# Reordering two periods of an attention-plus-MLP kernel, and moving one transpose from TensorE to DMA

## The chip, the cores and the metric

The kernel runs on one core of one Trainium2 chip. The metric is the device time of one execution in microseconds. Executions agree within some 0.3%. The experiments were timed in five or six rounds against the kernel before, on the same chip, and a trace of one execution of each is read beside the times. In the text PE is TensorE, DVE is VectorE, ACT is ScalarE, POOL is GpSimd, SP is SyncE, whose queue issues DMAs here. PSUM is the memory that PE writes its results to, a bank a part of it.

## The reference

Attention of 8 heads with a window of 96 positions, 8 global positions and a linear bias, followed by a two-layer MLP whose activation is a scaled and shifted square of relu:

```python
scores = scale * np.matmul(q, k.transpose(0, 1, 3, 2))       # 4 x 8 x 768 x 768
keep = is_global | is_local                                  # 8 global, 96 local
scores = np.where(keep, scores + bias, -1e9)
a = softmax(scores)
x = (a @ v).transpose(0, 2, 1, 3).reshape(3072, 512)
r = np.maximum(x @ w_in, 0.0)                                # 512 -> 2048
out = (s * (r * r) + b) @ w_out                              # 2048 -> 512
```

(`softmax` stands for the reference's maximum, exponential and division.)

## The kernel before

The 3072 tokens are cut into 12 granules of 256. For each granule: loads by POOL (f32 to bf16), transposes of k and q by DMA, scores, exponentials, multiplication by a bias template, values, normalization, transpose of the result x to xT, first layer, square, second layer. The instruction order on each engine is written by hand. Granules 0 to 2 are a start; granules 3 and 4 go through `period`, and from granule 5 on `steady` repeats. P1(3,0) in the text is block 0 of granule 3's first layer, xT(3) is xT of granule 3. In the steady part the second layer is computed with 7 instead of 8 block products, for which differences of w_out (`W_tw`) and sums of activations (`W_sw`) are made on DVE.

```python
def XT_pe(j, eng="act", tag="pso"):         # x -> xT on PE, copied out by ACT
    ...
    nc.tensor.transpose(ps[...], xn[j][...], ident[:])     # 8 of them
    nc.scalar.copy(xT[j][:], ps[:])

def XT_dma(j):                              # x -> xT by two DMA transposes from SP
    for i in range(GB):
        nc.sync.dma_start_transpose(xT[j][:, :, i * P : (i + 1) * P], xn[j][:, i, :, :]...)

def XB(j):                                  # k and q of a granule, four DMA transposes from SP
    XBk(j); XBq(j)

def P1(j, fp, sq="dve", ...):               # one of 8 first-layer blocks: 8 matmuls, relu on ACT;
    ...                                     # the square on ACT, on DVE, or later on DVE by Q(j, fp)

def P2(j, c):                               # one of 8 second-layer blocks: 4 matmuls

def period(j, items, at, late=None, mid=()):               # granules 3 and 4
    SS(j, (0, 1))                           # scores, exponentials, multiplication of two head pairs
    run(items, at[0]); A(j, 0)              # A: values and normalization of a head pair
    run(items, at[1]); A(j, 1, "psh")
    run(list(mid), 100)
    SS(j, (2, 3))
    if j == 3:
        pace(pts[j, 2][0:1, 0, 0:1])        # POOL waits for the multiplied scores,
        load_granule(6)                     # then issues the six loads of granule 6
    ...
    VO(j + 1); XB(j + 2)
    if late is not None:
        run(items, 1); late(); XT_pe(j, "act", "psh")      # granule 3
```

`KO` and `VO` copy the k and v blocks of the next granule side by side, with the global positions put in.

The softmax here doesn't subtract the row's maximum and nothing guards it: scores larger than these inputs give would overflow.

## Time and profile before

| view | value |
|---|---|
| time, median of the 3 runs given first | 207.81 us (207.53 to 207.9) |
| span of the profiled execution | 205.9 us |
| busy: PE, DVE, ACT, POOL | 96%, 84%, 56%, 36% |
| scores of granule 5 start (PE timeline) | 76.05 us |

The DVE timeline of the kernel before (start in us, length in us, instruction): the two value copies made while POOL issues loads, and the same two one granule later, when it doesn't.

```profile
60.71 0.76 DVE L363 COPY vo<-vaug 128x1040 bf16<-128x1040 bf16 x1
61.50 0.83 DVE L366 COPY vo<-vaug 8x1040 bf16<-8x1040 bf16 x1
...
72.90 0.43 DVE L363 COPY vo<-vaug 128x1040 bf16<-128x1040 bf16 x1
73.37 0.43 DVE L366 COPY vo<-vaug 8x1040 bf16<-8x1040 bf16 x1
```

The same copy costs nearly twice as much at 61 us as at 73 us.

### The profile page before, as it was taken

How to read it: one execution, taken by the hardware profiler on the slowest of the kernel's cores; microseconds unless marked ns; L12 is line 12 of the kernel's file. 1: busy time of each engine (PE TensorE's matmuls, PEld its weight loads, DVE VectorE, ACT ScalarE, POOL GpSimd, SP SyncE). 2: the span in 40 equal slices, each digit the busy share in tenths (PEclk: the TensorE clock that was granted, in tenths of full speed). 3: DMA queues.
4: the chain of work that ended last, by engine and by line, in shares of the span. 5: the costliest groups of instructions: out<-in, count | busy, mean ns of one | idle time of the engine just before them, and what ended most of it. 6: DMA issues, size and time to landing. Idle time of an engine off the chain costs nothing.

```text
span 205.9 us, 5597 instructions
## 1 busy us (share of the span) xinstructions
PE 198.5 (96%) x2286; PEld 160.6 (78%) x2293; DVE 173.4 (84%) x415; ACT 115.9 (56%) x174; POOL 73.2 (36%) x98
## 2 busy tenths in 40 slices
PE   7988999999999999999999999999999999999993
PEld 2667776547766678988988988988988988988883
DVE  5897677699989989788799799788799799787693
ACT  5887588355878576536536536536446446424400
POOL 8993683848274019009009119019000000000000
PEclk9999999999999999999999999999999999999999
DMA  5999999999999969969999969999975140040022
GB/s 164 193 184 197 192 194 193 181 154 145 148 133 150 237 83 99 194 137 118 108 227 109 208 91 106 204 109 121 204 85 140 42 133 23 0 153 5 0 105 102
DMA packets 103962, 27.64 MB, mean 134 GB/s; under 512 B 91392, under 2 KB 102016, under 8 KB 103936
## 3 DMA queue, kind: packets, MB, share of 16 engines
q0 software_dynamic: 70976, 13.11, 83.5%
q1 hardware_dynamic: 31904, 13.64, 33.8%
q10 hardware_dynamic: 1056, 0.52, 0.9%
q8 instruction: 18, 0.29, 0.6%
q14 instruction: 8, 0.07, 0.2%
HBM read 27.26 MB, written 6.29 MB: 163 GB/s over the span
## 4 chain that ended last, share of the span: by engine, by line
PE 81%; DMA 5%; POOL 5%; DVE 4%; ACT 2%; issue 1%; SPq 0%; POOLq 0%; ACTq 0%
PE ps L552 37%; PE ps_w L735 15%; PE ps_wb L735 7%; PE ps L622 6%; PE ps_av L470 4%; PE ps_wa L735 4%; DMA w_in_bf<-in_moe_w_in_dram 4%; PE ps_s L414 4%; POOL vaug L112 2%; PE ps_2s L622 2%; DVE pt L441 2%; DMA xT<-xn 1%; DVE o_pr L660 1%; POOL w_in_bf L129 1%; ACT pt L427 1%
## 5 line engine op out<-in xcount | busy, mean ns | idle before, releaser
L552 PE MATMUL ps<-xT,w_in_bf 128*128 128x256 bf16 x768 | 96.5, 273 | 2.1 <-DMA w_in_bf<-in_moe_w_in_dram 1.2
L552 PEld LDWEIGHTS <-w_in_bf 128*128 128x128 bf16 x768 | 72.6, 98 | 13.0 <-DMA w_in_bf<-in_moe_w_in_dram 2.3
L570 ACT ACTIVATE gT<-ps 128x512 bf16<-128x512 f32 x72 | 43.1, 598 | 58.5 <-PE ps L552 56.4
L427 ACT ACTIVATE pt<-ps_s 128x1024 bf16<-128x1024 f32 (+1 forms) x48 | 43.0, 950 | 4.0 <-PE ps_s L414 4.0
L735 PEld LDWEIGHTS <-sw 128*128 128x128 bf16 x288 | 28.1, 98 | 3.4
L589 DVE TENSOR_TENSOR gT<-gT 128x512 bf16<-128x512 bf16 x73 | 27.6, 415 | 1.7 <-ACT gT L570 1.6
L112 POOL DMA_DIRECT2D vaug<-in_v_dram x24 | 21.6, 912 | 4.1 <-DMA w_out_bf<-in_moe_w_out_dram 1.7
L441 DVE TENSOR_TENSOR pt<-pt,tmpl 128x1024 bf16<-128x1024 bf16 x31 | 20.7, 686 | 2.1 <-ACT pt L427 2.1
L735 PEld LDWEIGHTS <-gT 128*128 128x128 bf16 x208 | 19.8, 98 | 3.2 <-issue 0.2
L488 DVE TENSOR_TENSOR xn<-ps_av,rc 128x256 bf16<-128x256 f32 x48 | 20.4, 424 | 1.7
L125 POOL COPY pdum<-xT 1x1 bf16<-1x1 bf16 x5 | 2.5, 509 | 50.5 <-DMA xT<-xn 50.5
L622 PE MATMUL ps<-w_out_bf,gT 128*128 128x512 bf16 x74 | 18.8, 379 | 0.4 <-issue 0.2
L735 PE MATMUL ps_w<-tw,sw 128*128 128x256 bf16 x144 | 18.7, 273 | 0.0
L745 DVE SCALAR_TENSOR_TENSOR u<-ps_w,s_bc,bvec 128x256 f32<-128x256 f32 x27 | 12.9, 479 | 6.4 <-PE ps_w L735 6.4
L470 PEld LDWEIGHTS <-pt 128*128 128x128 bf16 x352 | 15.4, 98 | 3.3 <-DVE pt L441 1.2
L568 ACT ACTIVATE gT<-ps 128x512 bf16<-128x512 f32 x23 | 13.6, 598 | 6.9 <-PE ps L552 6.7
L104 POOL DMA_DIRECT2D qnat<-in_q_dram x18 | 16.0, 904 | 2.8 <-DMA w_out_bf<-in_moe_w_out_dram 1.4
L104 POOL DMA_DIRECT2D knat<-in_k_dram x18 | 15.9, 892 | 1.8 <-issue 1.5
L470 PE MATMUL ps_av<-vaug,pt 128*128 128x65 bf16 x224 | 16.2, 193 | 0.2 <-DVE pt L441 0.2
L622 PEld LDWEIGHTS <-gT 128*128 128x128 bf16 x96 | 8.7, 97 | 8.1
L487 DVE RECIPROCAL rc<-ps_av 128x4 f32<-128x4 f32 x48 | 8.7, 181 | 6.6 <-PE ps_av L470 6.4
L414 PE MATMUL ps_s<-qT,kT 64*128 64x128 bf16 x224 | 12.5, 218 | 0.1
(102 smaller groups left out, 242.4 us busy)
## 6 DMA issues: line engine op xcount, KB each, us to landing
out_dram<-o_pr SPq DMA_DIRECT2D x10, 512.0 KB, 6.0
vaug<-in_v_dram POOLq DMA_DIRECT2D x24, 128.0 KB, 8.0
knat<-in_k_dram POOLq DMA_DIRECT2D x22, 128.0 KB, 6.5
qnat<-in_q_dram POOLq DMA_DIRECT2D x22, 128.0 KB, 8.0
w_in_bf<-in_moe_w_in_dram POOLq DMA_DIRECT2D x8, 256.0 KB, 8.3
w_out_bf<-in_moe_w_out_dram POOLq DMA_DIRECT2D x4, 512.0 KB, 9.8
out_dram<-o_pr SPq DMA_DIRECT2D x3, 256.0 KB, 2.5
raw<-in_q_dram ACTq DMA_DIRECT2D x2, 256.0 KB, 4.9
```

The lines of the kernel that those rows point to most:

```text
L104: nc.gpsimd.dma_start(t[:, i, :, :], src[b, :, sb * P : (sb + 1) * P, :].rearrange("h p d -> p h d"))
L112: nc.gpsimd.dma_start(vaug[b % 2][:, sb, :, 0:D], v[b, :, sb * P : (sb + 1) * P, :].rearrange("h p d -> p h d"),)
L414: nc.tensor.matmul(ps[:, hi, oc * P : (oc + 1) * P], lhsT=kt[r, :], rhs=qT[j][r, hp, i * P : (i + 1) * P], start=not biased, stop=not bias ...
L427: nc.scalar.activation(pt[:, :, 0:n], ps[:, :, 0:n], ACT.Exp, scale=QSCALE)
L441: nc.vector.tensor_tensor(x, x, m.unsqueeze(2).to_broadcast((P, 2, GB, 2 * P)), ALU.mult)
L470: nc.tensor.matmul(av[:, i, hi, :], lhsT=pt[:, hi, c * P : (c + 1) * P], rhs=vv, start=n_ == 0, stop=n_ == len(ops) - 1,)
L488: nc.vector.tensor_tensor(xn[j][:, :, 2 * hp : 2 * hp + 2, :], av[:, :, :, 0:D], rc[:].to_broadcast((P, GB, 2, D)), ALU.mult,)
L552: nc.tensor.matmul(ps[:, i, :], lhsT=w_in_bf[:, kc, fc * P : (fc + 1) * P], rhs=xT[j][:, kc, :], start=(kc == 0), stop=(kc == KC - 1),)
L570: nc.scalar.activation(gs.rearrange("p f (r t) -> p f r t", r=2), ps[:].rearrange("p f (t r) -> p f r t", r=2), ACT.Relu,)
L589: nc.vector.tensor_tensor(gs, gs, gs, ALU.mult)
L622: nc.tensor.matmul(po[j, tb], lhsT=gT[j][:, fc, tb * P : (tb + 1) * P], rhs=w_out_bf[:, fc, :], start=(fc == 0), stop=(fc == FC - 1),)
L735: nc.tensor.matmul(wt[j, ps], lhsT=lhs[:, f, :], rhs=rhs[:, f, :], start=first and f == 0, stop=f == HF - 1, skip_group_check=True,)
```

## The change

Its intent: free PE of eight transposes and ACT of their copy, and write out granules 3 and 4 in an order in which PE has other work while DVE catches up and the transposes land. Three squares of granule 3 move from ACT to DVE. The value copies are split so that the second-layer output, which frees a PSUM bank, comes between them. Output stores go in halves.

```diff
-    def VO(j):
+    def VO(j, part=None):                   # part 0: the block copy, part 1: the global positions
     def wsum_fin():
-        ps = ps_h.tile([P, DM], F32, name="ps_b", tag="psh")
+        ps = ps_av.tile([P, DM], F32, name="ps_b", tag="av")
     def P2_out(j, tb):
-        if tb == 1:
-            P2_store_all(j)
+        nc.sync.dma_start(out[t0 : t0 + P, :], o_sb)
     def W_store(j):
-        nc.sync.dma_start(W_rows(j), wt[j, "o"][:])
+        if j < W0 + 4:
+            for r in range(2):
+                nc.sync.dma_start(W_rows(j)[:, r, :], wt[j, "o"][:, r, :])
+        else:
+            nc.sync.dma_start(W_rows(j), wt[j, "o"][:])
-    P2b(0); P2b(1)                          # (lines joined)
-    for f in range(4):
-        P1(2, f, "act" if f % 2 else "late")
-    Q(2, 0); Q(2, 2)
-    period(3, [...], (3, 1, 3, 1), wsum_fin, ((W_tw, 3, 0, 4), (W_tw, 3, 4, 8)))
+    for c in range(3):
+        P2b(c)
+    P1(2, 0, "late"); P1(2, 1, "act")
+    SS(3, (0, 1))
+    P2_mm(1, 1, 3); P1(2, 2, "late"); P2_raw(1, 1); wsum_fin(); P1(2, 3, "act")
+    ...
+    pace(pts[3, 2][0:1, 0, 0:1]); load_granule(6)
+    P1(2, 6, "act"); P1(2, 7, "act"); P2(2, 0); A(3, 2); A(3, 3, "psh")
+    XT_dma(3)
+    KO(4); P2(2, 1); VO(4, 0); P2(2, 2); P2(2, 3); VO(4, 1)
+    XB(5)
+    SS(4, (0, 1)); P2(2, 4); P2(2, 5)
+    ...
+    P2_mm(2, 1, 3)
+    P1(3, 0, "late")                        # first use of xT of granule 3
+    ...
```

More of the change, by code (lines that the diff above doesn't have):

```diff
@@ L361, in VO @@
             return
-        vo = work.tile([P, GB, H, VW], BF16, name="vo", tag="vo", bufs=2)
-        nc.vector.tensor_copy(
-            vo[:, :, :, 0:65], vaug[b % 2][:, g * GB - 1 : (g + 1) * GB - 1, :, 0:65]
-        )
-        nc.vector.tensor_copy(
-            vo[0:NG, :, :, 0:65],
-            vaug[b % 2][0:NG, 0:1, :, 0:65].to_broadcast((NG, GB, H, 65)),
-        )
-        vos[j] = vo
+        if part != 1:
+            vos[j] = work.tile([P, GB, H, VW], BF16, name="vo", tag="vo", bufs=2)
+        vo = vos[j]
+        if part != 1:
+            nc.vector.tensor_copy(
+                vo[:, :, :, 0:65],
+                vaug[b % 2][:, g * GB - 1 : (g + 1) * GB - 1, :, 0:65],
+            )
+        if part != 0:
+            nc.vector.tensor_copy(
+                vo[0:NG, :, :, 0:65],
+                vaug[b % 2][0:NG, 0:1, :, 0:65].to_broadcast((NG, GB, H, 65)),
+            )
     sps = {}
@@ L647, in P2_out @@
         )
-        if tb == 1:
-            P2_store_all(j)
+        t0 = b * S + g * GT + tb * P
+        nc.sync.dma_start(out[t0 : t0 + P, :], o_sb)
     raw = {}
@@ L662, in P2_bias @@
             P2_store(j, tb)
-    def P2_store_all(j):
-        b, g = bg(j)
-        t0 = b * S + g * GT
-        nc.sync.dma_start(
-            out[t0 : t0 + GT, :].rearrange("(i p) c -> p i c", p=P), o_t[j][:]
-        )
     def P2_store(j, tb):
@@ L993, in P2b @@
             P2_raw(1, 1)
-    def period(j, items, at, late=None, mid=()):
-        SS(j, (0, 1))
-        run(items, at[0])
-        A(j, 0)
-        run(items, at[1])
-        A(j, 1, "psh")
-        run(list(mid), 100)
-        SS(j, (2, 3))
-        if j == 3:
-            pace(pts[j, 2][0:1, 0, 0:1])
-            load_granule(6)
-        run(items, at[2])
-        A(j, 2)
-        if at[3]:
-            KO(j + 1)
-        run(items, at[3])
-        A(j, 3, "psh")
-        if not at[3]:
-            KO(j + 1)
-        if late is None:
-            XT_dma(j)
-        if j + 1 < NJ:
-            VO(j + 1)
-        if j + 2 < NJ:
-            XB(j + 2)
-        if late is not None:
-            run(items, 1)
-            late()
-            XT_pe(j, "act", "psh")
-        run(items, 100)
@@ L1026 @@
-    P2b(0)
-    P2b(1)
-    for f in range(4):
-        P1(2, f, "act" if f % 2 else "late")
-    Q(2, 0)
-    Q(2, 2)
-    period(
-        3,
-        [
-            (P2b, 2),
-            (P2b, 3),
-            (P1, 2, 4),
-            (P1, 2, 5, "act"),
-            (P1, 2, 6, "act"),
-            (P1, 2, 7, "act"),
-            (P2, 2, 0),
-            (P2, 2, 1),
-            (P2, 2, 2),
-            (P2, 2, 3),
-            (P2_bias, 0, 0, False),
-            (P2_bias, 0, 1, False),
-            (P2_store_all, 0),
-        ],
-        (3, 1, 3, 1),
-        wsum_fin,
-        ((W_tw, 3, 0, 4), (W_tw, 3, 4, 8)),
-    )
+    for c in range(3):
+        P2b(c)
@@ new lines @@
+    P1(2, 0, "late")
+    P1(2, 1, "act")
+    SS(3, (0, 1))
+    P2_mm(1, 1, 3)
+    P1(2, 2, "late")
+    P2_raw(1, 1)
+    wsum_fin()
+    P1(2, 3, "act")
+    Q(2, 0)
+    P2_bias(0, 0)
+    P1(2, 4)
+    A(3, 0)
+    P1(2, 5, "act")
+    A(3, 1, "psh")
+    Q(2, 2)
+    W_tw(3, 0, 4)
+    for hp in (2, 3):
+        S_mm(3, hp)
+    for hp in (2, 3):
+        S_post(3, hp, mul=False)
+    S_mul(3, 2)
+    S_mul(3, 3)
+    W_tw(3, 4, 8)
+    pace(pts[3, 2][0:1, 0, 0:1])
+    load_granule(6)
@@ new lines @@
+    P1(2, 6, "act")
+    P1(2, 7, "act")
+    P2(2, 0)
+    A(3, 2)
+    A(3, 3, "psh")
+    XT_dma(3)
+    KO(4)
+    P2(2, 1)
+    VO(4, 0)
+    P2(2, 2)
+    P2(2, 3)
+    VO(4, 1)
+    XB(5)
+    SS(4, (0, 1))
+    P2(2, 4)
+    P2(2, 5)
+    P2_bias(0, 1)
+    W_tw(2, 0, 4)
+    A(4, 0)
+    P2(2, 6)
+    A(4, 1, "psh")
+    for hp in (2, 3):
+        S_mm(4, hp)
+    for hp in (2, 3):
+        S_post(4, hp, mul=False)
+    S_mul(4, 2)
+    P2_mm(2, 1, 3)
+    P1(3, 0, "late")
+    P2_bias(1, 0)
@@ L1054, in P1s @@
+    S_mul(4, 3)
+    W_tw(2, 4, 8)
+    A(4, 2)
+    P1(3, 1, "late")
+    A(4, 3, "scB")
+    XT_dma(4)
+    P2_out(2, 1)
+    Q(3, 0)
+    KO(5)
+    P1(3, 2, "late")
+    VO(5)
+    XB(6)
+    Q(3, 1)
+    P2_bias(1, 1, False)
+    P1(3, 3)
+    Q(3, 2)
+    P1(3, 4)
+    P1(3, 5)
+    W_tw(4, 0, 4)
+    P1(3, 6)
+    P1(3, 7)
+    flush()
+    W_sw(3, 3)
+    W_tw(4, 4, 8)
     def P1s(j, fp, n):
@@ L1139, in steady @@
         W_sw(m, 3)
-    for j in range(4, NJ):
-        m, l = j - 1, j - 2
-        if l < W0:
-            items = [(P1, m, 0, "act"), (P2, l, 4), (P1, m, 1), (W_tw, 2, 0, 4)]
-            items += [(P2, l, 5), (P2_bias, 1, 0)]
-            items += [(P1, m, 2, "late"), (P1, m, 3, "late"), (P2, l, 6), (Q, m, 2), (Q, m, 3)]
-            items += [(P1, m, 4, "act"), (P2, l, 7), (P1, m, 5, "act"), (P1, m, 6), (W_tw, 4, 0, 4), (P1, m, 7), (W_sw, m, 3), (flush,), (W_tw, 4, 4, 8)]
-            period(j, items, (4, 2, 3, 0), mid=((W_tw, 2, 4, 8), (P2_bias, 1, 1, False)))
-        else:
-            steady(j)
+    for j in range(5, NJ):
+        steady(j)
     l, m = NJ - 2, NJ - 1
```

## The prediction

> **What bounds the kernel now.** I read the page's busy shares, then the windows in steps of 4 us, then the chain that ended last, then the timelines of the engines around the two periods that the change rewrites (granules 3 and 4 of 12).
>
> ```profile
> PE 198.5 (96%) x2286; PEld 160.6 (78%) x2293; DVE 173.4 (84%) x415; ACT 115.9 (56%) x174; POOL 73.2 (36%) x98
> ```
>
> TensorE (PE) is the bound as a whole. The windows (us of busy time of each engine in 4 us, then clock, DMA share, GB/s) say where it is not:
>
> ```profile
> 60.00:64.00 4.00, 4.00 (x43) 2.49 (x42) 3.79 (x8) 2.34 (x4) 3.83 (x5) 1.00 2.00 149
> 64.00:68.00 4.00, 3.95 (x51) 2.65 (x51) 3.97 (x9) 2.82 (x5) 0.00 (x0) 1.00 1.93 160
> 68.00:72.00 4.00, 3.58 (x38) 2.45 (x38) 3.92 (x10) 2.62 (x4) 0.00 (x0) 1.00 1.69 259
> ...
> 84.00:88.00 4.00, 4.00 (x51) 3.64 (x49) 3.32 (x9) 1.85 (x4) 0.00 (x0) 1.00 1.72 222
> ```
>
> From 64 to 72 us VectorE (DVE, the third pair) is full and PE lacks 0.47 us; from 84 us on PE is full and DVE has slack. The chain agrees (start, length, what):
>
> ```profile
> 62.49 0.57 PE ps_s L414 x16
> 63.09 0.75 DVE o_pr L640
> 63.84 1.20 DVE o_pr L660 x2
> 65.04 1.20 DVE pt L441 x2
> 66.25 0.60 DVE tw L691
> ...
> 70.08 1.22 DVE pt L441 x2
> 71.34 0.42 PE ps_av L470 x8
> 71.76 0.87 PE ps L552 x8
> 72.63 0.88 PE ps L622 x4
> 73.75 2.51 DMA xT<-xn
> 76.66 1.01 ACT pt L427
> 77.72 1.03 PE ps_wa L735 x8
> 78.75 1.75 PE ps L552 x16
> ```
>
> It lies on DVE from 63 to 71 us, then on the DMA transpose of xT, and from 78.75 us on PE nearly alone until the end. So **a gain must be PE time won before 78.7 us**; after that each us earlier is a us off the end, as long as DVE keeps up.
>
> How much is there? From the first block of the second layer of granule 1, second half (45.6 us, PE timeline) to the first score matmul of granule 5 (76.05) is 30.4 us. Block lengths from the chain: second layer 4 matmuls 0.865, first layer 8 matmuls 0.875, scores of two head pairs 0.44 (granule 3) and 0.57 (granule 4), values of one pair 0.18 and 0.245 (timeline), sum for the bias 0.43, PE transpose of xT 0.45. That is 12 x 0.865 + 16 x 0.875 + 2 x 0.44 + 2 x 0.57 + 4 x 0.18 + 4 x 0.245 + 0.43 + 0.45 = 29.0 us. **Gaps: 1.4 us.** Another 0.25 us is lost where ps_wa waits for an exponential (77.72, where 77.47 was possible). With the 0.45 us of the PE transpose the ceiling is 2.1 us, 1.0% of 207.8. Over 2% faster is nearly out of reach.
>
> **What the Trainium skill says.** "Perfetto Trace Analysis", section Identifying the Most-Contended Engine: matmul busy time is a poor measure of the distance to the roofline, as matmuls are pipelined. The trace agrees: busy 198.5 of 205.9 us hides what the sum of blocks shows. "VectorE: DVE Perf Modes", section The DRAIN you can't avoid: the next DVE operation waits until the pipe is empty, so a list of DVE operations simply adds up. The trace nearly agrees: starts are 0.60 us apart for records of 0.68 us (the f32 addition at 69.40, its follower at 70.00); I add start-to-start times. "DMA: Bandwidth & Descriptors", section Queues, rings and completion order: each DMA engine takes turns between the queues that have work, packet by packet. So transposes from the SP queue share with the loads from POOL, and the trace shows it, from issue to landing, in the stretch 53 to 62 us (loads in flight) and 70 to 78 us (few):
>
> ```profile
> qT<-qnat SPq DMA_TRANSPOSE x3, 7.5
> ...
> xT<-xn SPq DMA_TRANSPOSE x2, 2.5
> ```
>
> No page tells what these will take in the new order.
>
> **The change, part by part.**
>
> (1) xT of granule 3 by DMA: removes 8 PE transposes (0.45 us of PE) and ACT's copy (1.01 us). It adds two SP transposes, issued some 1.25 us apart, and moves the first use of this xT much later: before, the first-layer block P1(3,0) follows within about 2 us of the transposes; now ten blocks lie between.
>
> (2) Same DVE operations in another order, with one addition: three squares of granule 3 that ACT did (0.53 us each there) now fall to DVE, 3 x 0.335 = 1.0 us (pitch from 82.48: 1.09 us record for three). DVE is the engine that is full here, so this eats part of the gain.
>
> (3) The two value copies (0.76 and 0.83 us beside POOL's load issues at 60.7, 0.43 each at 72.9) are set around the first second-layer output, so the pso bank is released one copy, 0.8 us, sooner. No operation more.
>
> (4) Stores: granule 0's and 2's outputs go as halves, and so do the stores of granules 3 to 6: seven more issues on SP of about 0.25 us, where PE is the bound and nothing waits for the output: **0**.
>
> I then walked both queues by hand from 52.4 us, where DVE finishes the same weight differences in both kernels. DVE: two multiplications 0.6 each, bvec 0.64, square 0.34, bias add 0.6, normalization 0.6, square 0.35, normalization 0.6 (now 56.8, the block before it ends on PE at 56.0), square, differences, two multiplications, differences: 59.7. Two normalizations: **60.9, and SP can issue the transposes of xT(3) at 61.0 and 62.25**. ko 0.55, first copy 0.75, second-layer output 0.7 (63.0; PE, ready at 62.7, starts the next second-layer block 0.3 us late), second copy 63.8, two multiplications 65.1, bias add 65.7, differences 66.3, two normalizations 67.5, multiplication, bias add, multiplication, differences 69.9.
> PE: from that second-layer block at 63.05, two blocks (64.8), values, block, values (66.15), scores (66.75), block: **P1(3,0) is due at 67.6**. Then values, block and values to 69.85, and six first-layer blocks: scores of granule 5 at 75.1 instead of 76.05, **0.95 us gained** if xT(3) has landed. DVE then has normalizations, output, ko and vo, eight squares, differences: its first multiplication for granule 5 ends at 78.85, 0.2 us later than now (78.66), since it carries the 1.0 us more. So DVE limits the next period for a moment: the values of granule 5's last pair end at about 85.6 instead of 86.34. **0.75 us gained** is left, and DVE's slack afterwards keeps it.
>
> **The rivals.**
> - *The transpose takes the place of the wait removed.* xT(3) is issued in the middle of granule 6's loads (POOL issues 58.5 to 64; DMA share 2.0). Before's transposes at 59.7 and 61.0 took 7.1 and 7.5 us, but behind two others; the ones at 93.0 and 102.7, without a queue ahead, took 5.2 and about 4. At 62.25 + 5.3 = 67.6 (my estimate) it is just in time. At 7 us it lands at 69.3: PE stalls 1.7 us and the time is some 208.6. In favour: loads as dense as anywhere. Against: the ring is just drained at 61.0 (granule 4's last transposes land about 60.8), and in 55 to 68 us a transpose landed every 1.9 us on average.
> - *DVE is the bound all along.* Then moving things gains nothing, and three squares more cost up to 1.0 us: 207.8 to 208.8. The DVE share of 3.92 to 3.97 of 4 in 64 to 72 speaks for it; the 1.9 us that DVE idles from 84 to 91 us speaks against a loss that lasts.
> - *All gaps close*: 207.8 - 2.1 = 205.7. It would need DVE to be ahead everywhere, which the walk doesn't show.
> - *kT and qT of granule 5 come late*, as their transposes now stand behind xT(3) and a store: issued from about 64 instead of 55.8, to land near 72 to 74 for uses at 72 and 75. It is close, perhaps a few tenths lost.
>
> **Range and chances.** Gain by the walk 0.75 us; I take off 0.3 for the chance of a late xT(3) and 0.1 for granule 5, and put 0.4 back because the walk charges each DVE copy at its slow rate and the order looks arranged around the landing. 207.81 - 0.75 = 207.06: I predict **207.0 us, 206.0 to 208.1**. The low end is most of the ceiling; the high end is a late transpose partly caught up. Faster by over 2% (below 203.7) lies outside the ceiling: 0.01. Slower by over 2% (above 212) would need a stall of 4 us: 0.02. Within 2%: 0.97.
>
> **What would show it.** Right: in the changed profile the scores of granule 5 start near 75.1 us and PE is full from then on; P1(3,0) follows its second-layer block with no gap; the chain leaves DVE before 70 us. The landing of the xT transposes issued near 61 is the number to read: under 5.4 us for the second confirms, 7 or more means a wait of PE on xT. Step (2) is wrong if ACT, not DVE, is what PE waits for between 66 and 72. The prediction fails if PE shows a gap over 1 us for kT or qT of granule 5, or if more is gained than 1.4 us, which would say that DVE's list is shorter than I added up.

## The result, and the profile after

The changed kernel took 207.97 us (median of 4 runs, 207.75 to 208.23), the kernel before 207.67 us (4 runs). The ratio is 1.0015, with a 95% interval of 0.9997 to 1.0034: the same, within 2%, and inside the predicted range of 206.0 to 208.1, but 1.0 us over the predicted 207.0; a gain of 0.8 us was forecast, and none came. (A ratio here is the mean time of one kernel's runs over that of the other's of the same rounds, so it is not quite the ratio of the medians.)

The windows of the changed kernel, with the columns of the prediction's first windows:

```profile
60.00:64.00 4.00, 3.71 (x32) 1.80 (x30) 3.63 (x9) 2.17 (x4) 4.00 (x6) 1.00 2.13 182
64.00:68.00 4.00, 4.00 (x46) 2.08 (x44) 3.54 (x9) 1.86 (x3) 0.53 (x1) 1.00 2.28 166
68.00:72.00 4.00, 3.23 (x42) 2.93 (x42) 3.67 (x9) 2.01 (x3) 0.00 (x0) 1.00 1.76 176
...
84.00:88.00 4.00, 4.00 (x51) 3.63 (x49) 3.28 (x9) 1.85 (x4) 0.82 (x1) 1.00 2.18 143
```

DVE is no longer full from 64 to 72 us (3.54 and 3.67 instead of 3.97 and 3.92). PE however lacks 0.77 us from 68 to 72, more than before. The chain says why:

```profile
43.26 7.18 DMA qT<-qnat
...
50.48 0.46 PE ps_s L418 x10
50.94 0.97 PE ps L626 x4
...
62.28 6.47 DMA xT<-xn
...
68.80 1.05 PE ps L556 x8
...
71.20 5.25 PE ps L556 x48
```

Two DMA transposes stand in it that were not there before: q of granule 3, landed at 50.44 us, and xT of granule 3, in flight from 62.28 to 68.75. The PE timeline of the changed kernel shows both waits (in brackets the idle time of PE and what ended it):

```profile
49.98 0.23 PE L418 MATMUL ps_s<-qT,kT 64*128 64x128 bf16 x2
50.48 0.46 PE L418 MATMUL ps_s<-qT,kT 64*128 64x128 bf16 x10 [0.27 <-DMA qT<-qnat]
50.87 1.04 PE L626 MATMUL ps<-w_out_bf,gT 128*128 128x512 bf16 x4
...
66.99 1.04 PE L626 MATMUL ps<-w_out_bf,gT 128*128 128x512 bf16 x4
68.80 1.05 PE L556 MATMUL ps<-xT,w_in_bf 128*128 128x256 bf16 x8 [0.77 <-DMA xT<-xn]
```

**The account.** The scores of granule 3 start at 49.98; undisturbed they take 0.44 us, and the next block could start at 50.42 instead of 50.87: 0.45 us lost (the bracket's 0.27 leaves out the overlap of the first two matmuls). The second-layer block at 66.99 fills PE for 0.87 us, to 67.86; P1(3,0), the first use of xT, starts at 68.80: 0.94 us lost. The scores of granule 5 start at 76.38 instead of 76.05. Without the two waits this would be 76.38 - 0.45 - 0.94 = 74.99. So **the new order wins 1.06 us of PE time, two waits for transposes take 1.39 back, and the net is 0.33 us later**, close to the 0.30 us between the medians. The 1.06 us is a subtraction; what is really gained when both waits are gone is measured in e6. From there to the end PE runs alike in both.

### The profile page after: what moved, and what is told of

Read it like the earlier page. It is cut to its first block, busy times and chain, and to the rows that moved or that the text cites. A ratio compares the mean times of both kernels' runs of the same rounds, so it can differ in the third digit from the quotient of the medians.

```text
span 206.3 us, 5604 instructions
## 1 busy us (share of the span) xinstructions
PE 198.4 (96%) x2285; PEld 160.3 (78%) x2285; DVE 174.2 (84%) x418; ACT 113.5 (55%) x170; POOL 76.6 (37%) x98
## 4 chain that ended last, share of the span: by engine, by line
PE 66%; DMA 21%; POOL 6%; ACT 2%; DVE 2%; issue 1%; POOLq 0%; ACTq 0%; SPq 0%; DVEq 0%
PE ps L556 33%; PE ps_w L732 15%; PE ps_wb L732 7%; DMA w_in_bf<-in_moe_w_in_dram 5%; DMA qnat<-in_q_dram 4%; DMA w_out_bf<-in_moe_w_out_dram 4%; PE ps_wa L732 4%; DMA qT<-qnat 3%; PE ps_av L474 3%; DMA xT<-xn 3%; PE ps_s L418 3%; POOL w_in_bf L129 2%; POOL vaug L112 2%; ACT pt L431 1%; ACT gT L574 1%
## 5 line engine op out<-in xcount | busy, mean ns | idle before, releaser
L593 DVE TENSOR_TENSOR gT<-gT 128x512 bf16<-128x512 bf16 x74 | 28.1, 416 | 1.7 <-ACT gT L574 1.6
L125 POOL COPY pdum<-xT 1x1 bf16<-1x1 bf16 x5 | 6.3, 1257 | 46.1 <-DMA xT<-xn 46.1
L626 PE MATMUL ps<-w_out_bf,gT 128*128 128x512 bf16 x80 | 19.3, 379 | 0.3 <-DVE o_pr L644 0.3
```

The source lines that it names most:

```text
L593: nc.vector.tensor_tensor(gs, gs, gs, ALU.mult)
L626: nc.tensor.matmul(po[j, tb], lhsT=gT[j][:, fc, tb * P : (tb + 1) * P], rhs=w_out_bf[:, fc, :], start=(fc == 0), stop=(fc == FC - 1),)
```

## The experiments

The theory: PE's order is as good as predicted, but the DMA engines are loaded in this stretch, so a transpose that is used earlier, or issued in the middle of loads, turns into a wait. The main rival: DVE is the bound all along. Twelve kernels ran, in three calls of four; each is compared with the kernel before of its own call. "Landing" is the time from a transpose's issue to its landing, the median of the two of one xT where nothing else is said.

| kernel | median us | ratio to before, 95% interval | landing of xT(3) | scores of granule 5 start |
|---|---|---|---|---|
| changed | 207.97 | 1.0015 (0.9997 to 1.0034) | 6.4 | 76.38 |
| e1 xT by PE, new order | 208.17 | 1.0024 (1.0012 to 1.0036) | none | 76.67 |
| e2 later loads | 207.89 | 1.0001 (0.9989 to 1.0014) | 2.9 | 76.61 (after a wait) |
| e3 before, xT by DMA | 216.52 | 1.0432 (1.0419 to 1.0445) | 6.5 | 84.07 |
| e4 scores later | 208.04 | 1.0015 (1.0001 to 1.0030) | 6.5 | 75.89 |
| e5 xT by PE, placed better | 207.33 | 0.9980 (0.9967 to 0.9993) | none | 75.68 |
| e6 transposes spread | 206.80 | 0.9955 (0.9943 to 0.9966) | 3.4 | 75.30 |
| e7 squares on ACT | 208.38 | 1.0028 (1.0013 to 1.0043) | 6.2 | 76.62 |
| e8 whole stores | 209.00 | 1.0056 (1.0044 to 1.0068) | 6.5 | 77.15 |
| e9 changed, again | 207.88 | 1.0021 (1.0003 to 1.0040) | 5.8 | 76.06 |
| e10 e6, whole stores | 207.18 | 0.9975 (0.9960 to 0.9990) | 3.8 | 75.08 |
| e11 e6, whole copies | 206.81 | 0.9966 (0.9954 to 0.9978) | 4.8 | 74.98 |
| e12 before, later loads | 207.44 | 0.9988 (0.9976 to 1.0000) | none | 75.51 |

The traces start a little differently each time: the last scores of granule 2, before any of these edits, lie between 35.8 and 36.9 us. A shift of some tenths in the last column is no effect by itself.

### e1: xT of granule 3 by PE again, in the new order

```diff
-    XT_dma(3)
     KO(4); P2(2, 1); VO(4, 0); P2(2, 2); P2(2, 3)
+    XT_pe(3, "act", "psh")
```

> The changed kernel with one part undone: xT of granule 3 is again transposed on PE (8 transposes, ACT copy), placed after the first-layer-independent block P2(2,3); the new order, the split copies and stores stay. Theory (the DMA transpose lands late and PE waits for it): the 0.94 us wait of PE at 67.9 us goes, 0.45 us of PE work comes back; the scores of granule 5 start at about 75.9 instead of 76.4 us, and the time is about 0.5 us under the changed kernel, 207.3 to 207.6. Rival (DVE is the bound all along): DVE has the same list, so the scores start as before near 76.4 and the time stays at 208.0 or gets worse by the 0.45 us, 208.4.

Measured: 208.17 us, no gain. The wait on xT was gone, as expected; but the miss teaches something. The ACT timeline and the PE timeline of e1:

```profile
63.34 1.01 ACT L510 COPY xT<-ps_x 128x1024 bf16<-128x1024 bf16 x1 [1.90 <-PE ps_x L504]
64.25 1.95 ACT L431 ACTIVATE pt<-ps_s 128x1024 bf16<-128x1024 f32 x2
...
66.06 0.20 PE L474 MATMUL ps_av<-vaug,pt 128*128 128x65 bf16 x1 [0.37 <-DVE pt L445]
```

ACT's copy of xT holds up the exponentials of granule 4 (64.25; 62.80 in the changed kernel), these hold up DVE's multiplication and that the values on PE. One wait was exchanged for another, besides the 0.45 us of transposes. By its time alone e1 would have spoken for the DVE rival; the trace shows that DVE itself waited 1.2 us for ACT there (0.4 us in the changed kernel). The wait for q of granule 3 was also longer, 0.68 us instead of 0.45. e5 places the same thing better.

### e2: the loads of granule 6 later

```diff
-    pace(pts[3, 2][0:1, 0, 0:1])
-    load_granule(6)
     ...
     SS(4, (0, 1))
+    pace(pts[4, 0][0:1, 0, 0:1])
+    load_granule(6)
```

> The changed kernel with only the loads of granule 6 started later: POOL's pacing copy waits for the first multiplied scores of granule 4 (about 64.5 us) instead of those of granule 3 (58.7 us), so no load is issued while xT of granule 3 is transposed by DMA. Theory (the loads in flight are what slows the transposes): their landing falls from 6.3 to 6.5 us to 2.5 to 4 us, PE's wait on xT (0.94 us) vanishes, scores of granule 5 start near 75.4 us, time about 207.0 (0.9 to 1.0 under the changed kernel, 0.6 under the one before), unless the later loads now slow the transposes of granule 5 and a new wait appears there. Rival (the transposes are slow by themselves at this place, or because of the ones before them in their own queue): landing stays at 6 us or more and the time at 208.0. Rival (DVE bound): landing falls, but the time stays within 0.3 us of 208.0.

The transposes of xT(3) in the trace, from issue to landing, first in the changed kernel, then in e2, both in the stretch from 62 to 64 us:

```profile
xT<-xn SPq DMA_TRANSPOSE x2, 6.4
```

```profile
xT<-xn SPq DMA_TRANSPOSE x2, 2.9
```

**With no load being issued they take 2.9 instead of 6.4 us, and PE's wait on xT is gone.** That settles the main cause of the landing: the loads. (Without loads it is still not one number: in e6, e10 and e11, where the k transposes of granule 5 were issued a few us earlier, the same transposes took 3.4 to 4.8 us.) Yet the time was 207.89 us, because the second half of the expectation came true. The PE timeline of e2:

```profile
75.65 0.23 PE L418 MATMUL ps_s<-qT,kT 64*128 64x128 bf16 x2
76.61 0.23 PE L418 MATMUL ps_s<-qT,kT 64*128 64x128 bf16 x2 [0.72 <-DMA qT<-qnat]
```

The loads now lie beside the q transposes of granule 5, whose second took 7.1 us from 69.4 and landed at 76.56. The wait moved by eight microseconds and about kept its size. In this trace, which started 0.46 us sooner, PE also lost 1.08 us to q of granule 3, which landed at 50.61, instead of 0.45.

### e3: the DMA transpose alone, in the old order

```diff
 def period(...):                            # of the kernel before
-        if late is None:
-            XT_dma(j)
+        XT_dma(j)
     ...
             late()
-            XT_pe(j, "act", "psh")
```

> The kernel before with one part of the change alone: xT of granule 3 by DMA instead of PE, issued right after the normalization of granule 3, in the old order (first use two blocks later, at about 62.5 us). Theory: issued near 60.8 us, the second transpose lands near 68.4 us; PE waits some 5 to 6 us for it, part of which DVE uses to catch up with its list; the time is 3 to 5 us over the kernel before (about 211 to 212.5). Rival (the transposes take the 2.5 us that they take at 72 us): they land at 65, and the time is within 1.5 us of the kernel before.

Measured: 216.52 us, 8.9 us over the kernel before. The landing was as expected (6.5 us), the loss nearly twice that. The PE timeline and the windows of e3 (PE is the first pair, the granted clock the third number from the right) show what I had left out:

```profile
69.32 1.87 PE L552 MATMUL ps<-xT,w_in_bf 128*128 128x256 bf16 x8 [6.52 <-DMA xT<-xn]
...
69.00:71.00 2.00, 1.68 (x9) 1.21 (x10) 0.00 (x0) 0.00 (x0) 0.00 (x0) 0.50 1.38 233
71.00:73.00 2.00, 2.00 (x7) 0.83 (x6) 0.00 (x0) 1.23 (x2) 0.00 (x0) 0.50 0.77 268
73.00:75.00 2.00, 2.00 (x18) 1.39 (x17) 0.19 (x2) 0.47 (x1) 0.00 (x0) 0.69 0.03 10
```

The clock fell during the wait of 6.5 us (0.86 granted from 66 to 68 us, 0.50 from 68 to 69); PE then runs at half of it for about 5 us, and eight matmuls take 1.87 us instead of 1.05. The Trainium skill says so ("TensorE: Matmul & The Clock Gate", section What's actually happening: the throttled state comes back after an idle window of about 3.4 us and leaves after one of activity); this trace agrees, with 0.50 granted from 69 to 73 us. The change's new order is thus no extra: without it, this transpose by DMA costs 4%.

### e4: the scores of granule 3 one block later

```diff
-    SS(3, (0, 1))
     P2_mm(1, 1, 3)
+    SS(3, (0, 1))
```

> The changed kernel with the last second-layer block of granule 1 put ahead of the first scores of granule 3 instead of behind them (one swap of two program lines). In the changed kernel these scores sit in the middle waiting about 0.27 us for the DMA transposes of q of granule 3, which land at 50.4 us. Theory: the wait goes and everything up to 67.9 us comes 0.3 us earlier, but xT of granule 3 is issued only as much earlier as DVE allows; if its landing moves with it, the time falls by 0.3 us to about 207.7; if the landing of xT is set by the loads, PE only waits longer for xT and the time stays at 208.0.

In its trace the wait for q is gone and the first-layer block behind the two starts at 51.03 instead of 51.74, but xT(3) again lands 6.7 us after its second issue, and PE waits 0.99 us for it. The scores of granule 5 start at 75.89, 0.49 us sooner than in the changed kernel, in an execution that also started some 0.3 us sooner. The timed runs say nothing of it: 208.04 us, with a spread of 207.57 to 208.69. So the wait is real, but its removal alone is not shown to gain time.

### e5: xT by PE in ACT's idle time, k and q of granule 5 early

```diff
+    P2_mm(1, 1, 3) before SS(3, (0, 1)), as in e4
+    XB(5)                                   # behind P2_bias(0, 0); removed behind VO(4, 1)
-    XT_dma(3)
     SS(4, (0, 1)); P2(2, 4); P2(2, 5)
+    XT_pe(3, "act", "psh")
```

> A version that the first four runs point to: the changed kernel with (a) the scores of granule 3 behind the last second-layer block of granule 1, (b) xT of granule 3 by PE, now in ACT's idle stretch between the two pairs of exponentials of granule 4 (after the second-layer block P2(2,5)), so that its copy doesn't hold up an exponential as in e1, and (c) the transposes of k and q of granule 5 issued early again, as in the kernel before. Theory (what the new order gains is 0.6 us of PE time, lost to waits for transposes on a loaded DMA): no wait on a DMA is left; against the changed kernel minus 0.94 (xT) minus 0.3 to 0.5 (q of granule 3) plus 0.45 (PE transposes), scores of granule 5 near 75.4 us, time 207.0 to 207.3, about 0.3% under the kernel before. Rival (DVE is the bound between 60 and 76 us): PE waits for DVE instead, the scores of granule 5 stay at 76 or later and the time at 207.7 or more.

Measured: 207.33 us, ratio 0.9980 (0.9967 to 0.9993), 0.03 us above the band that I gave, but 0.64 us under the changed kernel's median and clear of the kernel before. No wait on a DMA is left in its list of waits. In the ACT timeline the copy now stands at 65.40 us, between the two pairs of exponentials at 62.56 and 67.08. DVE has the same list as in the changed kernel, so the rival "DVE is the bound" falls here for the first time.

### e6: all transposes kept on the DMA, but spread

```diff
+    P2_mm(1, 1, 3) before SS(3, (0, 1)), as in e4
+    loads of granule 6 behind SS(4, (0, 1)), as in e2
     P2_bias(0, 0)
+    XBk(5)                                  # k of granule 5 ahead of xT(3)
     ...
-    XB(5)
+    XBq(5)
```

> The changed kernel with the transposes kept on the DMA but spread: scores of granule 3 later (e4), loads of granule 6 later (e2), and the k transposes of granule 5 issued before those of xT of granule 3, so that its q transposes start about 3 us earlier than in e2. Theory: xT of granule 3 and q of granule 5 are in time (no PE wait at 68 and 76), scores of granule 5 near 75.2 us; but the loads of granule 6 now lie beside the xT transposes of granule 4 (5.4 to 5.8 us in e2), which land near 78.5 us where PE wants them at 77.5, so about 0.8 us comes back as a wait there: time 207.2 to 207.7. Rival (the DMA is no shared resource, each wait is its own): no new wait, time 206.8.

Measured: **206.80 us, ratio 0.9955 (0.9943 to 0.9966): with e11 the best of all, 1.2 us under the changed kernel and 0.9 us under the kernel before.** That is better than I expected of it: the wait on the xT transposes of granule 4 did not come. They took 4.9 us, issued from 71.42 us on; POOL, which paces its next loads by them, went on at 77.28, and PE first wanted them at 78.00 (I had put the need at 77.5). The time is the one that I had written for the rival "the DMA is no shared resource", but e2 speaks against that rival, and so does the xT of granule 4 here: 4.9 us among the loads, 3.0 in the changed kernel. There was just time enough. The list of PE's waits from 45 us to the end of e6 has one line, and no DMA:

```profile
PE ps L626 <- DVE o_pr L644: 0.3, 1, 0.3
```

The later loads have a second effect, in the DVE timeline of e6, where POOL issues nothing from 55 to 64.9 us:

```profile
61.28 0.43 DVE L366 COPY vo<-vaug 128x1040 bf16<-128x1040 bf16 x1
62.28 0.75 DVE L644 SCALAR_TENSOR_TENSOR o_pr<-ps,s_bc,bvec 128x512 f32<-128x512 f32 x1 [0.57 <-PE ps L626]
62.95 0.42 DVE L371 COPY vo<-vaug 8x1040 bf16<-8x1040 bf16 x1
```

The copies take 0.43 us; in the changed kernel, beside POOL's load issues, 0.73 and 0.78. The Trainium skill has the mechanism ("SBUF — State Buffer", section Who interferes with whom: copies in the two-port mode and POOL lock a shared pair of ports against each other, and the later one waits). The durations agree with it; no trace here shows the lock itself, or the mode of these copies.

### e7: the three squares back on ACT

```diff
-    P1(3, 0, "late"); P1(3, 1, "late"); P1(3, 2, "late")     # squared on DVE by Q
+    P1(3, 0, "act");  P1(3, 1, "act");  P1(3, 2, "act")
```

> The changed kernel with the three squares of granule 3 that the change moved to DVE given back to ACT (first-layer blocks 0 to 2). My prediction charged 1.0 us of DVE for them. Theory (from 68.8 us on PE is full and DVE is behind nothing that PE waits for): DVE's first multiplication for granule 5 ends up to 1.0 us sooner, but PE's start of the scores of granule 5 stays near 76.4 us and the time at 208.0 (within 0.2). Rival (DVE is the bound): the time falls by 0.5 to 1.0 us.

Measured: 208.38 us, ratio 1.0028 (1.0013 to 1.0043); the control e9 has 1.0021 (1.0003 to 1.0040). That is 0.2 us above the band that I gave. Taking 1.0 us from DVE gained nothing, which is what the theory says and the rival denies. It is not a clean test, though. ACT was in the chain, relu and square alternating, from 69.8 to 73.9 us; and DVE's first multiplication for granule 5 began at 78.90, as without the edit (78.92). DVE's waits from 68 to 79 us in e7 (us in total, times, longest) show where its time went:

```profile
DVE ko L338 <- DMA kT<-knat: 0.8, 1, 0.8
```

That is another transpose of granule 5, which the changed kernel issues late; DVE came to it earlier and waited. In the changed kernel this line is missing.

### e8: output stores whole again

```diff
     def P2_out(j, tb):
+        if tb == 1:                         # one store of both halves
     def W_store(j):
-        if j < W0 + 4:
+        if False:
```

> The changed kernel with the output stores of granules 2 to 6 whole again (one store each, as before, instead of two halves). Theory: nothing on PE waits for a store and SP has room: time 208.0, within 0.2, scores of granule 5 within 0.2 us of 76.4. Rival (the extra issues on SP, or the half stores beside the transposes, delay the transposes): the xT of granule 3 lands sooner and the time falls by some tenths.

Measured: 209.00 us, ratio 1.0056: 0.35% (0.7 us) over the control e9 by the ratios, with intervals that don't meet (1.0044 to 1.0068, and 1.0003 to 1.0040). This is a miss. In its trace PE waits 1.16 us for xT(3) and 0.46 us for q of granule 3; the scores of granule 5 start at 77.15, and from there on PE runs as in the changed kernel. But the wait for q stands at 50.9 us, before any store that the edit touches, and the median of the two landings of xT(3), 6.5 us, hides that the second, for which PE waits, took 0.39 us longer than the 6.47 of the changed kernel:

```profile
62.66 6.86 DMA xT<-xn
```

The 0.77 us by which the scores of granule 5 are later in e8's trace are 0.19 of a later start, 0.19 of q of granule 3 and 0.39 of this landing. So landings make the loss; that the stores make the landings later isn't shown. The edit's store of 63.6 us is missing between the transposes of xT(3) and those of k of granule 5, which is the only difference that I see before the wait. Whether this explains a part stays open.

### e9: the changed kernel once more

> The changed kernel itself, unaltered, as a control beside the three others of this call: e7 and e8 came out 0.4 and 1.0 us over the changed kernel's first four runs, which were on another chip and in other rounds. Theory (its edge over or under the kernel before is set by when DMA transposes land, which differs a little between executions and builds): 207.8 to 208.4, ratio to the kernel before 1.001 to 1.003. If it comes out near 208.8 here, the 1.0 us of e8 was no effect of the stores.

Measured: 207.88 us, with single executions from 207.59 to 208.94. In its trace xT(3) landed after 5.8 us and PE's wait shrank to 0.33 us. A spread over 1.35 us would fit a time that hangs on landings, but that isn't shown: of the kernels in whose traces PE waits for no DMA, e11 spread over 0.23 us, e6 over 0.55 and e10 over 0.96.

### e10 and e11: stores, and copies, in one piece in e6

```diff
 e10:  the edit of e8, on e6
 e11: -    VO(4, 0); P2(2, 2); P2(2, 3); VO(4, 1)
      +    VO(4);    P2(2, 2); P2(2, 3)
```

> The version of e6 with the output stores of granules 2 to 6 whole again: the same edit as e8, where no transpose is awaited. Theory (stores cost PE nothing by themselves; in e8 they only shifted the landing of transposes that PE was waiting for): within 0.3 us of e6's 206.8. Rival (whole stores delay SP's queue or hold the output buffers that DVE writes): 0.5 us or more over e6.

> The version of e6 with the value copies of granule 4 in one piece again, ahead of the first second-layer output. In e6 no load is issued by POOL at that time and the copies take 0.43 us each instead of 0.73 to 0.78, and DVE idles 0.57 us before the output. Theory: the second copy fits into that idle time, so the split is worth nothing here: within 0.2 us of e6's 206.8. Rival (the split is worth its 0.75 us wherever it stands, as the prediction had it): PE gets the bank 0.4 to 0.7 us later and the time is 207.2 or more.

e10: 207.18 us, 0.38 us over e6's median and 0.37 over e11, with intervals of 0.9960 to 0.9990 and 0.9954 to 0.9978 that overlap; the 0.38 lies 0.08 us outside my band, and not yet in the rival's. Whole stores cost at most some tenths where no transpose is awaited; zero is not shown, and neither is a cost. e11: 206.81 us. The split of the copies is worth nothing in e6. Its DVE timeline:

```profile
60.97 0.43 DVE L366 COPY vo<-vaug 128x1040 bf16<-128x1040 bf16 x1
61.44 0.43 DVE L371 COPY vo<-vaug 8x1040 bf16<-8x1040 bf16 x1
61.97 0.75 DVE L644 SCALAR_TENSOR_TENSOR o_pr<-ps,s_bc,bvec 128x512 f32<-128x512 f32 x1
```

Both copies fit in before the output, which still comes right after PE's block.

### e12: the later loads alone, in the kernel before

```diff
 def period(...):
-        if j == 3: pace(pts[j, 2]...); load_granule(6)       # behind SS(j, (2, 3))
+        if j == 4: pace(pts[j, 0]...); load_granule(6)       # behind SS(j, (0, 1))
```

> The kernel before with one thing from e6 that the change doesn't contain: the loads of granule 6 start behind the first multiplied scores of granule 4 (about 66 us) instead of those of granule 3. Is e6's gain the new order at all, or only the later loads? Theory: DVE's copies at 60 to 62 us get faster (0.43 instead of 0.76 and 0.83, and 0.18 for 0.43), so DVE's chain starts about 0.6 us earlier, but the xT transposes of granule 4 (72.5 us) now lie in the loads, land near 78 instead of 76.3, and give some 0.5 us back: 207.2 to 207.8. Rival (the later loads alone make e6): 206.8 to 207.0.

Measured: 207.44 us, ratio 0.9988 (0.9976 to 1.0000), as expected: 0.12% is gained by the later loads alone (0.24% at the end of the interval), against 0.34% and 0.45% in e11 and e6, whose intervals begin at 0.22% and 0.34%. DVE's output starts at 62.55 us instead of 63.09, the xT transposes of granule 4 take 4.8 us instead of 2.5, and PE waits 0.17 us for them: 0.54 us are won by the scores of granule 5 (75.51), and 0.19 are left at their second half (81.60 instead of 81.79). So by the times most of e6's gain is the new order, once its waits are gone; the later loads serve to remove them.

## Why the prediction was right or wrong

Right, within its range and class; the centre was 1.0 us too low. The direction was wrong: the gain of 0.75 us that the working arrives at did not come. The result lies in the range because its upper end was set for a late transpose partly caught up, which came true; that a second wait, which nobody had foreseen (0.45 us), was nearly made up by what the order gained beyond the working (0.31 us) is luck. Of the signs, the chain left DVE early (at 62.2 us) and PE was full from the scores of granule 5 on; but these started at 76.38 and not near 75.1, and P1(3,0) did not follow without a gap.

- **The ceiling and where to look.** Right. All that differs for PE lies before 78.7 us; from the scores of granule 5 on PE runs alike in both, and the best version found gains 0.9 us of the 2.1 us allowed. One reading was too literal: the step of the old chain on xT of granule 4 (73.75 to 76.26 us) held PE up nowhere, as PE's timeline has no gap there from 71.34 to 76.6 us.
- **The walk up to the transposes.** Right: xT(3) was to be issued at 61.0 and 62.25, and was at 61.03 and 62.28; P1(3,0) was due at 67.6, and PE was free for it at 67.86. The walk quotes the Trainium skill ("VectorE: DVE Perf Modes", The DRAIN you can't avoid) for a wait until the pipe is empty; the same section adds that an operation which isn't held starts earlier. The trace has starts 0.60 us apart for records of 0.68, and these start-to-start times, which the walk used, are what added up.
- **"62.25 + 5.3 = 67.6 ... just in time."** This is the term that was mis-sized. The second landing took 6.47 us, not 5.3, so the first rival came true in part: 0.94 us of waiting. I had taken 5.2 and 4 us from places where loads were beginning or ending, and set aside the 7.1 and 7.5 us of nearly the same moment because two transposes stood ahead of them. e2 shows that the loads count most: 2.9 us without them.
- **A wait that the prediction lacks.** The walk began at 52.4 us. The change also moves the first scores of granule 3 about 0.9 us up, to 49.98, and their q landed only at 50.44: 0.45 us lost. I checked q and k of granule 5, not of granule 3. In the changed kernel those of granule 5 cost PE nothing; they became the wait in e2.
- **Part 2, 1.0 us more on DVE, and "DVE limits the next period".** The operations are there: DVE's first multiplication for granule 5 started at 78.92 us in the changed kernel, 0.86 us later than in the kernel before (78.06), where the walk had 0.2. But PE shows no wait for it. The reduction from 0.95 to 0.75 us was not needed: e6, with the same DVE list, gains 0.9 us in time. e7 points the same way, less cleanly.
- **Part 3, the bank one copy sooner.** PE waited 0.29 us for the output with the split, as predicted (0.3). What the split saves in the changed kernel was not tried alone; in e6 it is nothing (e11).
- **Part 4, stores: 0.** Not confirmed. (The seven more issues are six: 13 stores of 256 KB and more in the page before, 19 after.) e8 stands 0.7 us over the control; its trace puts the loss on landings and doesn't tie these to the stores. e10 is undecided.
- **The sum.** I took off 0.4 us for both risks and put 0.4 us back because the order "looks arranged around the landing". That was a guess about the author, not a number from a row; without it the centre would have been 207.5 and the miss 0.5 us. Net of it all, the walk's gain of 0.75 us against the measured loss of 0.33 is a difference of 1.08: 1.39 us of waits not charged, less 0.31 that the order gained beyond 0.75.

## What to carry to other kernels

When an order is tightened by a microsecond, ask of every operand that arrives by DMA when it lands, not only of the one that the change moves: the time gained on TensorE here went whole into two such waits. Here one and the same transpose took 2.9 us without loads being issued and 6.4 us among them, so read its duration from the same moment of the trace, and move the loads before moving the transpose. When a wait disappears and the time stays, look for the wait that took its place; here it stood eight microseconds later.

## What the Trainium skill lacked or had wrong

- How long a DMA transpose takes beside loads is on no page: "DMA: Bandwidth & Descriptors" says that the queues take turns, but not what that costs. The transposes of one xT took a median of 2.9 us without loads being issued (e2) and 6.4 us in the middle of them (the changed kernel); in e6, e10 and e11, without loads but with other transposes shortly before, 3.4 to 4.8 us.
- "SBUF — State Buffer" tells of the lock between a two-port copy and POOL, but not of its price for a whole copy: 0.43 us without and 0.73 to 0.83 us beside POOL's load issues.
